# PSUM tiles of one bank, values loaded first, and stores issued from ScalarE, in a pooled-attention and mixture-of-depths kernel

## The chip, the cores and the metric

The kernel runs on one core of one Trainium2 chip. The metric is the device time of one execution in microseconds. The core has a matrix engine (TensorE, "PE" in the profile, with "PEld" for its weight loads), VectorE (DVE), ScalarE (ACT), GpSimd (POOL) and SyncE (SP), each with its own in-order queue. Matmuls write to PSUM, a memory of eight banks of 512 float32 values in each of 128 partitions; everything else is in SBUF. SP, ACT and POOL can issue transfers (DMAs).

## What is computed

Eight batches of an attention with pooled keys and values, followed by a feed-forward block that only the best 128 of 576 rows pass through. In short:

```python
# q, k, v: (8, 8, 576, 64)
k_p = k.reshape(B, H, 72, 8, D).mean(axis=3); v_p = v.reshape(B, H, 72, 8, D).mean(axis=3)
scores = scale * q @ k_p^T                       # per head (576, 72)
attn = softmax(scores);  x = attn @ v_p          # bridged to x: (8, 576, 512)
# mixture of depths, per batch
s = x @ w_gate                                   # (576,)
top = the 128 rows of largest s
h = relu(x[top] @ w1);  y = h @ w2               # 512 -> 1024 -> 512
out = x;  out[top] = x[top] + sigmoid(s[top]) * y
```

## The kernel before

`direct_path` is what runs (`general_path` is code for inputs out of range and is skipped). Per batch there are these stages, each with its name in the code and the engine it is on:

- Loads of k, q and v from SP (`load`, line 285 for all DMAs of SP). The values are folded in halves: of the 128 partitions of the tile `vr`, 112 are plain and 16 get a second key's rows added by an accumulating DMA that POOL issues (line 367).
- Pooling of k (L380, L381) and its transposition and that of q on DVE (L386 to L401); pooling of v, with the gate's product and sum (L443 to L455).
- `scores` (L419): four groups t of matmuls into the PSUM tile `pS`; `ex` (L429) takes the exponential into `et`.
- `attend` (L470): five groups c of matmuls into two banks of the PSUM tile `pB` (one bank for c = 4). `zs` (L485, L486, ACT) copies the row sums out, `norm` (L492, L493, DVE) divides and writes `xs`; then `xs` is stored to the output (32 stores of 256 KB, 16 of 64 KB).
- `rank`: the row scores are transposed on PE (`spread`, L542), copied by ACT (L547), compared on DVE (five times L554), turned into one-hot rows (L559); a matmul (`pick`, L568) gives the row numbers, DVE reads them (L573, L574), POOL makes indices (L578) and gathers the chosen rows from the stored output (L579).
- `dense`: `turn` (L596) transposes them, ACT copies (L598), `up` (L605) is 64 pieces of the first product in two halves g, `relu` (L610, ACT) follows each half, `down` (L614) the second product, `end` (L619, DVE) the sum, `put` (L623, POOL) scatters the rows.

The order of all work on each engine is written out before the program is built. Every stage calls `add` with a cost, what it reads and writes, a priority and, for PSUM, the banks it may take; `Plan.place` runs a small model of the five engines, picks at each step the ready stage of the best priority, and sorts all by the modelled start. Waits between engines are then put in by the framework, which follows each tile. A DMA of SP or ACT also uses one of eight semaphores (DMAHW0 to DMAHW7) in turn, and is issued only after the DMA that used the same semaphore before it has landed.

`pB` is one tile of four banks: 0 and 1 for the attends, 2 and 3 for the jobs (spread, pick, turn, up, down). `pS` is one tile of four banks, in which the plan sees two slots of 128 columns, both in each of the banks.

Of the kernel before, what the change touches and what calls it, by code (L numbers as in the profile page):

```python
# [165 lines left out]
def direct_path(ctx, tc, q, k, v, moe_w_gate, moe_w1, moe_w2, moe_capacity, out, flag):  # L166
# [11 lines left out]
    NC = 5  # L178
# [84 lines left out]
    pB = psum.tile([128, 4, 512], FT, name="pB")  # L263
# [28 lines left out]
    def opening():  # L292
# [51 lines left out]
    def load_kq(b):  # L344
        p = 100 * b
        src = k[b].rearrange("h (g t) d -> (h g) t d", g=G)
        cuts = ((0, 20), (20, 36)) if b == 0 else ((0, 36),)
        for n, (a, z) in enumerate(cuts):
            load(KR[:, a:z], src[:, a:z], 128 * 256 * (z - a), p + n,
                (), [("KR", n)] if b == 0 else [("KR", 0), ("KR", 1)])  # L350
        src = q[b].rearrange("h (g t) d -> (h g) t d", g=G)
        for h, (a, z) in enumerate(HALF):
            load(QR[b % 2][h], src[:, a:z], 128 * 256 * (z - a), p + 2, (), [("QR", b % 2, h)])

    def load_v(b):
        p = 100 * b + 3
        i = b % 2
        x = VR[i]

        def rows(key, n, step):  # L360
            return bass.AP(tensor=v.tensor, offset=v.offset + b * H * S * D + key * W * D,
                           ap=[[step * W * D, n], [S * D, H], [1, W * D]])
        load(x[TWO:128], rows(TWO, 128 - TWO, 2), (128 - TWO) * 8192, p, (), [("VRb", i)])
        load(x[0:TWO], rows(0, TWO, 1), TWO * 8192, p, (), [("VRa", i)])

        def more():
            nc.gpsimd.dma_start(out=x[TWO:128], in_=rows(TWO + 1, 128 - TWO, 2), accum_op=OP.add)  # L367
        add("POOL", 1.0, more, (), [("VRb", i)], p - 100, nbytes=(128 - TWO) * 8192)
# [89 lines left out]
    def attend(b, c):  # L458
        i = b % 2
        et = ET[c][b % NB[c]]  # L460
        slot = ("acc", b, c)
        vkeys = [(x, i, n) for x in ("VPd", "VPg") for n in range(2)]

        def go():
            bank = plan.bank[slot][0]
            for s in range(2):
                for m in range(NP):
                    for u in range(ROWS[c] // 64):
                        w, d, y = (u, s, m) if c < 4 else (m // 2, 0, 2 * s + m % 2)
                        nc.tensor.matmul(pB[64 * w : 64 * w + 64, bank + d, E * y : E * y + E],  # L470
                                         et[:, 2 * m + s, 64 * u : 64 * u + 64], VP[i][:, 2 * m + s, :], start=True, stop=True)
        add("PE", 1.05 if c < 4 else 0.6, go, [("ET", c, b % NB[c])] + vkeys, [slot], 100 * b + 5 + c,
            takes=(slot, ((ACC2 if b < 2 else ACC) if c < 4 else (ONE2 if b < 2 else ONE))))
# [3 lines left out]
        def acc():  # L477
            bank = plan.bank[slot][0]
            if c < 4:
                return pB[:, bank : bank + 2, 0 : NP * E].rearrange("p s (m d) -> p s m d", d=E)  # L480
            return pB[:, bank, 0 : NP * E].rearrange("p (s m d) -> p s m d", s=2, d=E)

        def zs():
            o = acc()
            nc.scalar.activation(ZA[:, b, z0 : z0 + nz].rearrange("p (s m) -> p s m", s=2), o[:, :, :, D], AF.Identity, bias=eps)  # L485
            nc.scalar.copy(out=SS[i][:, c, 0:nz].rearrange("p (s m) -> p s m", s=2), in_=o[:, :, :, D + 1])  # L486
        add("ACT", 0.45, zs, [slot], [("Z", b, c), ("SS", i, c)], 100 * b - 35)

# [13 lines left out]
        if c < 4:  # L502
            dma(rows[:, TC * c : TC * c + TC], XS[i][c], 128 * 2048, 100 * b + 4,
                [("XS", i, c)], [("ROWS", b, c, 0)], then=kept)
        else:
            for w in range(2):
                dma(rows[:, TC * c : TG, 256 * w : 256 * w + 256], XS[i][c][64 * w : 64 * w + 64],
                    64 * 1024, 100 * b + 4, [("XS", i, c)], [("ROWS", b, c, w)], then=kept)

    def rank(b):  # L510
# [23 lines left out]
        for half, (a, z) in enumerate(((0, 3), (3, NC))):  # L534
# [11 lines left out]
            def keep(a=a, w=w, slot=slot):  # L546
                nc.scalar.copy(out=SR[:, OFF[a] : OFF[a] + w], in_=pB[:, plan.bank[slot][0], 0:w])  # L547
# [16 lines left out]
        def pick():  # L564
            bank = plan.bank[slot][0]
            for c in range(NC):
                n = ROWS[c]
                nc.tensor.matmul(pB[0:cap, bank, 0:5], OH[0:n, c, :], AUX[i][0:n, c, :], start=(c == 0), stop=(c == NC - 1))  # L568
        add("PE", 0.4, pick, ["OH", ("AUX", i)], [slot], p - 70, takes=(slot, JOB))

        def token():
            got = pB[0:cap, plan.bank[slot][0]]
# [4 lines left out]
        def index():  # L577
# [6 lines left out]
            [("IX", x), ("XR", x)], p - 90, nbytes=262144, mark=b)  # L584
# [4 lines left out]
    def dense(b):  # L589
# [4 lines left out]
        def turn():  # L594
            for d in range(DB):
                nc.tensor.transpose(pB[:, plan.bank[ts][0], cap * d : cap * d + cap], XR[x][:, 128 * d : 128 * d + 128], ident[:cap, :cap])  # L596
        add("PE", 0.55, turn, [("XR", x), "ident"], [ts], p - 15, takes=(ts, JOB))
        add("ACT", 0.6, lambda: nc.scalar.copy(out=XG[i].rearrange("p d n -> p (d n)"), in_=pB[:, plan.bank[ts][0], 0 : DB * cap]),  # L598
            [ts], [("XG", i)], p - 5000, gives=(ts,))
        for g in range(2):  # L600
            for f in range(FB // 2):
                def up(f=f, g=g):
                    bank = plan.bank[us[g]][0]
                    for d in range(DB):
                        nc.tensor.matmul(pB[:, bank, cap * f : cap * f + cap], w1[g][:, d, 128 * f : 128 * f + 128],  # L605
# [3 lines left out]
            def relu(g=g):  # L609
                nc.scalar.activation(HT[i][g].rearrange("p f n -> p (f n)"), pB[:, plan.bank[us[g]][0], 0 : FB // 2 * cap], AF.Relu)  # L610
            add("ACT", 0.65, relu, [us[g]], [("HT", i, g)], p - 5000, gives=(us[g],))
        for f in range(FB):
            def down(f=f):
                nc.tensor.matmul(pB[0:cap, plan.bank[ds][0], :], HT[i][f // 4][:, f % 4, :], w2[f // 4][:, f % 4, :],  # L614
# [3 lines left out]
        def end():  # L618
            nc.vector.scalar_tensor_tensor(Y[i], pB[0:cap, plan.bank[ds][0], :], GV[x], XR[x], op0=OP.mult, op1=OP.add)  # L619
# [7 lines left out]
        add("POOL", 1.1, put, [("Y", i), ("IX", x)], [("OUT", b)], p - 5000, nbytes=262144, mark=b)  # L627
# [9 lines left out]
    def range_test():  # L637
# [11 lines left out]
        add("PE", 0.2, lambda: nc.tensor.matmul(pB[0:1, plan.bank[slot][0], 0:2], ones, seen, start=True, stop=True),  # L649
            ["seen0", "seen1", "ones"], [slot], 2050, takes=(slot, JOB))  # L650

        def verdict():
            nc.vector.scalar_tensor_tensor(match, pB[0:1, plan.bank[slot][0], 0:2], 1.0, want, op0=OP.mult, op1=OP.is_equal, accum_out=good)
# [16 lines left out]
    for b in range(2):  # L670
        load_kq(b)
        load_v(b)
        if b == 0:
            load_gate()
        else:
            weights()
        front(b)
    for b in range(B):
        dense(b)
        if b + 2 < B:  # L680
            load_kq(b + 2)
            load_v(b + 2)
# [359 lines left out]
```

## Time and profile before

| | us |
|---|---|
| three runs | 357.27, 348.56, 357.25; median 357.25 |
| profiled execution | 351.87 |
| its span, first to last instruction | 350.1 |

The profile gives for each engine when an instruction ran and what ended the idle time before it. A name such as `xs L493` is the instruction of that line that writes `xs`. A wait for several semaphores is put down to the one that came last. The granted clock of TensorE is given as a share of full speed: 1.00 is 2.4 GHz, 0.50 is 1.2 GHz.

### The profile page before, as it was taken

The numbers are of one execution on the slowest core, as the hardware profiler recorded it, in microseconds if no ns is written. First come the engines' busy times: TensorE is split into PE (matmuls) and PEld (weight loads), VectorE is DVE, ScalarE is ACT, GpSimd is POOL, SyncE is SP. The second block draws the span as 40 slices with busy tenths as digits, with TensorE's granted clock in tenths as the row PEclk, the third lists the DMA queues.
The fourth block names the chain that finished last, engine by engine and source line by source line (L and its number), as shares of the span: only waits on it lengthen the run. The fifth ranks groups of instructions, "written<-read, shape, count | busy, mean of one in ns | idle before, by whom it ended". The sixth has DMA issues, their size and how long they took to land. (4 is left out here: it accounts for less than half of the span.)

```text
span 350.1 us, 6979 instructions
## 1 busy us (share of the span) xinstructions
PE 246.8 (70%) x2942; PEld 180.4 (52%) x2942; DVE 147.2 (42%) x323; ACT 72.1 (21%) x178; POOL 111.2 (32%) x166
## 2 busy tenths in 40 slices
PE   8546620969677886767686886766857887979890
PEld 3435610858543765633575653653446637464740
DVE  7473269576444885374564136124322151000000
ACT  1313030344112533120244311022010101010000
POOL 2104068857490856553541211110020002010101
PEclk9965875899899999999999999898965999999996
DMA  8999997979825938815421210311121001000000
GB/s 287 291 261 309 404 288 281 222 254 278 301 59 133 323 94 224 301 33 128 139 51 40 84 47 31 91 47 31 30 91 38 9 0 61 2 30 0 32 6 33
DMA packets 22663, 46.93 MB, mean 134 GB/s; under 512 B 1888, under 2 KB 12128, under 8 KB 21728
## 3 DMA queue, kind: packets, MB, share of 16 engines
q1 hardware_dynamic: 20192, 41.16, 38.7%
q0 software_dynamic: 2432, 5.24, 5.9%
q8 instruction: 25, 0.41, 0.5%
q14 instruction: 14, 0.11, 0.1%
HBM read 34.87 MB, written 11.53 MB: 133 GB/s over the span
## 5 line engine op out<-in xcount | busy, mean ns | idle before, releaser
L605 PE MATMUL pB<-xg,w 128*128 128x128 f32 x512 | 74.1, 299 | 21.9 <-DVE xs L493 13.1
L605 PEld LDWEIGHTS pB<-xg,w 128*128 128x128 f32 x512 | 65.8, 206 | 29.8 <-DVE xs L493 16.2
L614 PE MATMUL pB<-w,ht 128*128 128x512 f32 x128 | 63.8, 624 | 12.8 <-ACT ht L610 4.3
L470 PE MATMUL pB<-vp,et 128*64 128x66 f32 x1152 | 46.1, 237 | 15.8 <-DVE xs L493 8.0
L419 PE MATMUL pS<-qt,kt 32*128 32x128 f32 (+1 forms) x1024 | 43.7, 319 | 17.6 <-ACT et L429 11.4
L470 PEld LDWEIGHTS pB<-vp,et 128*64 128x64 f32 x1152 | 40.9, 149 | 23.9 <-DVE xs L493 9.0
L554 DVE SCALAR_TENSOR_TENSOR cmp<-sr,sc,lat 128x576 bf16<-128x576 f32 (+1 forms) x40 | 41.8, 1044 | 21.2 <-ACT sr L547 20.0
L419 PEld LDWEIGHTS pS<-qt,kt 32*128 32x128 f32 x1024 | 37.9, 208 | 22.5 <-ACT et L429 14.3
L429 ACT ACTIVATE et<-pS 128x1024 f32<-128x1024 f32 (+1 forms) x40 | 36.6, 942 | 40.5 <-PE pS L419 40.5
L614 PEld LDWEIGHTS pB<-w,ht 128*128 128x128 f32 x128 | 22.2, 193 | 43.0 <-issue 16.5
L493 DVE TENSOR_TENSOR xs<-pB,rz 128x512 f32<-128x512 f32 (+1 forms) x40 | 25.5, 638 | 24.7 <-PE pB L614 9.3
L492 DVE RECIPROCAL rz<-za 128x8 f32<-128x8 f32 (+1 forms) x40 | 7.8, 196 | 66.5 <-ACT za L485 66.4
L623 POOL DMA_INDIRECT out_dram<-y,ix x8 | 8.7, 1091 | 71.4 <-DVE y L619 51.1
L619 DVE SCALAR_TENSOR_TENSOR y<-pB,gv,xr 128x512 f32<-128x512 f32 x8 | 6.0, 749 | 51.1 <-PE pB L605 19.2
L485 ACT ACTIVATE za<-pB,eps 128x8 f32<-128x8 f32 (+1 forms) x40 | 10.7, 268 | 79.4 <-PE pB L605 35.9
L380 POOL TENSOR_TENSOR kr<-kr 128x640 f32<-128x640 f32 (+1 forms) x12 | 18.4, 1534 | 13.5 <-DMA kr<-in_k_dram 13.5
L443 POOL TENSOR_TENSOR vr<-vr 128x512 f32<-128x512 f32 x15 | 21.3, 1420 | 2.6 <-DMA vr<-in_v_dram 2.6
L401 DVE STREAM_TRANSPOSE qt<-qr 128x1024 f32<-128x1024 f32 (+1 forms) x16 | 21.7, 1366 | 0.4 <-DMA qr<-in_q_dram 0.4
L610 ACT ACTIVATE ht<-pB 128x512 f32<-128x512 f32 x16 | 9.6, 597 | 57.7 <-PE pB L605 32.0
L578 POOL TENSOR_SCALAR ix<-tk 128x1 int32<-128x1 f32 x8 | 2.3, 289 | 58.2 <-DVE gv L574 50.5
L527 POOL CAST aux<-sc 128x5 bf16<-128x5 f32 x8 | 1.6, 198 | 44.8 <-DVE sc L522 44.8
L367 POOL DMA_DIRECT2D vr<-in_v_dram x8 | 7.8, 979 | 21.5 <-DMA vr<-in_v_dram 21.4
(74 smaller groups left out, 172.2 us busy)
## 6 DMA issues: line engine op xcount, KB each, us to landing
out_dram<-xs SPq DMA_DIRECT2D x32, 256.0 KB, 3.4
kr<-in_k_dram SPq DMA_DIRECT2D x7, 1152.0 KB, 11.3
vr<-in_v_dram SPq DMA_DIRECT2D x8, 896.0 KB, 7.7
qr<-in_q_dram SPq DMA_DIRECT2D x8, 640.0 KB, 8.8
qr<-in_q_dram SPq DMA_DIRECT2D x8, 512.0 KB, 10.8
w<-in_moe_w_dram SPq DMA_DIRECT2D x4, 1024.0 KB, 17.8
vr<-in_v_dram SPq DMA_DIRECT2D x8, 128.0 KB, 3.6
vr<-in_v_dram POOLq DMA_DIRECT2D x8, 128.0 KB, 8.3
```

The costliest lines, as they stand in the source:

```text
L380: e.tensor_tensor(out=x[:, a:z, 0:2], in0=x[:, a:z, 0:2], in1=x[:, a:z, 2:4], op=OP.add)
L401: nc.vector.transpose(out=QT[b % 2][h].rearrange("p j s (t g) -> p t (j s) g", g=G), in_=QR[b % 2][h].rearrange("p t (j s g) -> p t (j s) ...
L419: nc.tensor.matmul(pS[:, i, 256 * s + y : 256 * s + y + n], KT[b % 2][p, j, s, :], QT[b % 2][h][p, j, s, x : x + n], start=(j == 0), stop= ...
L429: nc.scalar.activation(ET[c][b % NB[c]].rearrange("p n (g t) -> p n g t", g=G), pS.rearrange("p i (s x) -> p (i s) x", s=2)[:, :, y : y + ...
L443: e.tensor_tensor(out=x[:, a:z, 0:2], in0=x[:, a:z, 0:2], in1=x[:, a:z, 2:4], op=OP.add)
L470: nc.tensor.matmul(pB[64 * w : 64 * w + 64, bank + d, E * y : E * y + E], et[:, 2 * m + s, 64 * u : 64 * u + 64], VP[i][:, 2 * m + s, :], ...
L485: nc.scalar.activation(ZA[:, b, z0 : z0 + nz].rearrange("p (s m) -> p s m", s=2), o[:, :, :, D], AF.Identity, bias=eps)
L493: nc.vector.tensor_tensor(out=XS[i][c].rearrange("p (m s d) -> p s m d", s=2, d=D), in0=o[:, :, :, 0:D], in1=rz.rearrange("p (s m one) -> ...
L554: nc.vector.scalar_tensor_tensor(cmp[0:n], SR[0:n], SC[i][0:n, c : c + 1], LAT[0:n, LAST - OFF[c] : LAST - OFF[c] + S], op0=OP.subtract, o ...
L605: nc.tensor.matmul(pB[:, bank, cap * f : cap * f + cap], w1[g][:, d, 128 * f : 128 * f + 128], XG[i][:, d, :], start=(d == 0), stop=(d == ...
L610: nc.scalar.activation(HT[i][g].rearrange("p f n -> p (f n)"), pB[:, plan.bank[us[g]][0], 0 : FB // 2 * cap], AF.Relu)
L614: nc.tensor.matmul(pB[0:cap, plan.bank[ds][0], :], HT[i][f // 4][:, f % 4, :], w2[f // 4][:, f % 4, :], start=(f == 0), stop=(f == FB - 1))
```

## The change

Three things are changed, and the plan's description of them with them.

PSUM: `pB` is split into `pA` (two banks, one tile, for the attends) and `pJ0`, `pJ1` (one bank each, for the jobs). The plan sees four slots: 0 is `pA`, 1 and 2 are the jobs, 3 is the whole of `pS`, so one group of scores at a time. In batches 0 and 1 an attend may also take both job banks; c = 4 may take `pA` or a job bank. Where an attend lies in two tiles, `zs` and `norm` are issued once for each.

Loads: the values' small piece comes first in each batch, then k, then q and the rest of v (for batch 0 v before q). The plan sees the accumulating DMA with another cost.

Stores: the stores of `xs` are issued by ACT, with a priority ahead of the loads' old place; the plan gives them a cost of 0.3 on ACT and no bytes.

```diff
-    plan.free = {x: 0.0 for x in range(6)}
-    SIDE, BOTH = [(4,), (5,)], [(4, 5)]
-    ACC, ACC2 = [(0, 1)], [(0, 1), (2, 3)]
-    ONE, ONE2 = [(0,), (1,)], [(0,), (1,), (2,), (3,)]
-    JOB = [(2,), (3,)]
+    plan.free = {x: 0.0 for x in range(4)}
+    ACC, ACC2 = [(0,)], [(0,), (1, 2)]
+    ONE = [(0,), (1,), (2,)]
+    JOB = [(1,), (2,)]
+    SIDE = [(3,)]
...
-    pB = psum.tile([128, 4, 512], FT, name="pB")
+    pA = psum.tile([128, 2, 512], FT, name="pA")
+    pJ = [psum.tile([128, 512], FT, name=f"pJ{i}") for i in range(2)]
...
-        return add(eng, 0.06 if eng == "SP" else 1.0, go, reads, writes, prio, nbytes=nbytes, after=after)
+        if eng == "SP":
+            return add(eng, 0.06, go, reads, writes, prio, nbytes=nbytes, after=after)
+        return add(eng, 0.3, go, reads, writes, prio, late=2.5, after=after)
...
-        add("POOL", 1.0, more, (), [("VRb", i)], p - 100, nbytes=(128 - TWO) * 8192)
+        add("POOL", 1.0, more, (), [("VRb", i)], 100 * b - 97, late=4.0)
...
-            y = off()
-                        nc.tensor.matmul(pS[:, i, 256 * s + y : 256 * s + y + n], KT[b % 2][p, j, s, :],
+                        nc.tensor.matmul(pS[:, i, 256 * s : 256 * s + n], KT[b % 2][p, j, s, :],
-            takes=(slot, SIDE if t < 3 else BOTH))
+            takes=(slot, SIDE))
...
-            takes=(slot, ((ACC2 if b < 2 else ACC) if c < 4 else (ONE2 if b < 2 else ONE))))
+            takes=(slot, ((ACC2 if b < 2 else ACC) if c < 4 else ONE)))
...
-            dma(rows[:, TC * c : TC * c + TC], XS[i][c], 128 * 2048, 100 * b + 4,
-                [("XS", i, c)], [("ROWS", b, c, 0)], then=kept)
+            dma(rows[:, TC * c : TC * c + TC], XS[i][c], 128 * 2048, 100 * b - 30,
+                [("XS", i, c)], [("ROWS", b, c, 0)], then=kept, eng="ACT")
...
-            [("IX", x), ("XR", x)], p - 90, nbytes=262144, mark=b)
+            [("IX", x), ("XR", x)], p - 90, late=3.5, mark=b)
...
-    for b in range(2):
-        load_kq(b)
-        load_v(b)
-        if b == 0:
-            load_gate()
-        else:
-            weights()
-        front(b)
+    load_v1(0)
+    load_k(0)
+    load_v2(0)
+    load_q(0)
+    load_gate()
+    front(0)
+    load_v1(1)
+    load_k(1)
+    load_q(1)
+    load_v2(1)
+    weights()
+    front(1)
```

The change moves work on every engine. Three places follow; line numbers of the changed kernel are some lines higher (L470 becomes L478, L605 becomes L615, L614 becomes L624, L419 becomes L424, L485 becomes L495, L429 becomes L434).

On PE, the attends of batch 2 and the down pieces of batch 0 among them, before (`vp0` and `et` belong to batch 2, `ht00` and `ht01` are the two halves of batch 0's hidden rows; in brackets the engines or DMA semaphores that the row waits for):

```order
L470 MATMUL pB_160<-vp0_90,et20_86 64x66 x16
L614 MATMUL pB_160<-w20_143,ht00_135 128x512 [waits DMAHW6_49,Activation_49]
L614 MATMUL pB_160<-w20_143,ht00_135 128x512 [waits Activation_49]
L614 MATMUL pB_160<-w20_143,ht00_135 128x512 [waits DVE_49]
L470 MATMUL pB_160<-vp0_90,et30_88 64x66 x16
L614 MATMUL pB_160<-w20_143,ht00_135 128x512
L614 MATMUL pB_160<-w21_144,ht01_136 128x512 [waits DMAHW7_49,DVE_49]
L470 MATMUL pB_160<-vp0_90,et40_89 64x66 x8
```

And in the changed kernel:

```order
L624 MATMUL pJ1_162<-w20_143,ht00_135 128x512
L478 MATMUL pA_160<-vp0_90,et10_84 64x66 [waits DVE_49]
L478 MATMUL pA_160<-vp0_90,et10_84 64x66 x15
L424 MATMUL pS_159<-qt01_79,kt0_76 128x192 [waits Activation_49]
L424 MATMUL pS_159<-qt01_79,kt0_76 128x192 x15
L624 MATMUL pJ1_162<-w21_144,ht01_136 128x512 [waits DMAHW1_49]
L478 MATMUL pA_160<-vp0_90,et20_86 64x66 [waits DVE_49]
L478 MATMUL pA_160<-vp0_90,et20_86 64x66 x15
L624 MATMUL pJ1_162<-w21_144,ht01_136 128x512
L478 MATMUL pJ0_161<-vp0_90,et40_89 64x66 [waits Activation_49]
```

The waits for DVE and ACT stood at the down pieces, and now stand at the attends and the scores.

On POOL, the first batches' values, before (`vr0`, `vp0` are batch 0's, `vr1` batch 1's; the two DMAs are the accumulating ones):

```order
L367 DMA vr0_72<-in_v_dram 16x8x256 [waits DMAHW4_49]
L367 DMA vr1_73<-in_v_dram 16x8x256 [waits DMAHW2_49]
L443 TENSOR_TENSOR vr0_72<-vr0_72 128x4x128 [waits DMAHW5_49,DMASW0_49]
L451 TENSOR_TENSOR vr0_72<-vp0_90,wg_92 128x4x64 [waits DMAHW6_49,DVE_49]
L447 TENSOR_TENSOR vp0_90<-vr0_72 128x4x64 [waits Pool_49]
```

And in the changed kernel:

```order
L372 DMA vr0_72<-in_v_dram 16x8x256 [waits DMAHW0_49]
L448 TENSOR_TENSOR vr0_72<-vr0_72 128x4x128 [waits DMAHW3_49,DMASW0_49]
L452 TENSOR_TENSOR vp0_90<-vr0_72 128x4x64 [waits Pool_49]
L456 TENSOR_TENSOR vr0_72<-vp0_90,wg_92 128x4x64 [waits DMAHW6_49,DVE_49]
L456 TENSOR_TENSOR vr0_72<-vp0_90,wg_92 128x4x64 [waits Pool_49]
L372 DMA vr1_73<-in_v_dram 16x8x256 [waits DMAHW7_49]
```

Batch 1's accumulating DMA has moved from ahead of batch 0's pooling to behind it.

On ACT, the end of batch 0's attention, before (`et01` is batch 1's first exponential, `sr` the copy for batch 0's rank):

```order
L485 ACTIVATE za_145<-pB_160,eps_146 128x4 [waits DVE_49,PE_49]
L486 COPY ss0_103<-pB_160 128x4
L429 ACTIVATE et40_89<-pS_159 128x512 [waits Activation_49]
L518 COPY ss0_103<-ss0_103 64x4 [waits DVE_49,Activation_49]
L547 COPY sr_112<-pB_160 128x384 [waits PE_49]
```

And in the changed kernel:

```order
L289 DMA out_0_dram<-xs03_96 16x8x512 [waits DMAHW4_49,DVE_49]
L434 ACTIVATE et01_83<-pS_159 128x1024 [waits PE_49]
L528 COPY ss0_103<-ss0_103 64x4 [waits DVE_49,Activation_49]
L289 DMA out_0_dram<-xs04_97 16x4x256 [waits DMAHW6_49]
L289 DMA out_0_dram<-xs04_97 16x4x256 [waits DMAHW0_49]
L434 ACTIVATE et11_85<-pS_159 128x1024 [waits PE_49]
L557 COPY sr_112<-pJ0_161 128x384 [waits PE_49]
```

Stores now stand between the exponentials, each behind a DMA semaphore: DMAHW4, DMAHW6 and DMAHW0 were last used by the first three of the four weight loads.

## Rows read from the trace of the kernel before

**Rows 1.** Windows, PE alone: stretch, length, PE busy (instructions), granted clock, DMA.
```profile
0.00:81.87 81.87, 46.66 (x832) 0.79 0.96 290
81.87:342.05 260.18, 200.12 (x2115) 0.95 0.30 88
255.00:275.00 20.00, 14.68 (x101) 0.57 0.20 60
```

**Rows 2.** Waits of PE: line, waited for: us in total, times, longest.
```profile
PE pB L605 <- DVE xs L493: 13.1, 11, 1.5
...
PE pB L614 <- ACT ht L610: 4.3, 6, 0.7
PE pB L605 <- ACT ht L610: 3.5, 5, 0.7
...
PE pB L614 <- DVE xs L493: 3.1, 3, 1.5
PE pB L568 <- DVE xs L493: 3.0, 3, 1.4
PE pB L614 <- ACT ss L486: 2.9, 7, 0.4
PE pB L542 <- DVE xs L493: 2.8, 3, 1.3
PE pB L470 <- ACT ht L610: 2.7, 4, 0.7
PE pB L596 <- DVE xs L493: 2.6, 2, 1.5
...
PE pB L470 <- DVE y L619: 2.3, 2, 1.5
...
PE pB L596 <- DVE gv L574: 0.4, 1, 0.4
```

**Rows 3.** Waits of PE again: scores on the exponential.
```profile
PE pS L419 <- ACT et L429: 11.4, 10, 2.1
```

**Rows 4.** Timeline of PE, 222 to 230: start, us, instruction, [idle before, releaser].
```profile
224.97 1.15 PE L470 MATMUL pB<-vp,et 128*64 128x66 f32 x32
226.05 1.16 PE L605 MATMUL pB<-xg,w 128*128 128x128 f32 x8
228.70 1.16 PE L605 MATMUL pB<-xg,w 128*128 128x128 f32 x8 [1.49 <-DVE xs L493]
```

**Rows 5.** Timeline of ACT, the same stretch.
```profile
227.25 0.27 ACT L485 ACTIVATE za<-pB,eps 128x8 f32<-128x8 f32 x1 [4.50 <-PE pB L605]
```

**Rows 6.** Timeline of DVE, the same stretch.
```profile
227.95 0.69 DVE L493 TENSOR_TENSOR xs<-pB,rz 128x512 f32<-128x512 f32 x1 [0.20 <-DVE rz L492]
```

**Rows 7.** Timeline of the opening, all engines, 0 to 60.
```profile
10.70 17.21 SPq L285 DMA_DIRECT2D w<-in_moe_w_dram  x4
11.00 1.45 POOL L367 DMA_DIRECT2D vr<-in_v_dram  x1 [8.25 <-DMA vr<-in_v_dram]
...
25.64 0.88 POOL L367 DMA_DIRECT2D vr<-in_v_dram  x1 [13.18 <-DMA vr<-in_v_dram]
26.24 1.57 POOL L443 TENSOR_TENSOR vr<-vr 128x512 f32<-128x512 f32 x1
...
36.83 2.26 PE L470 MATMUL pB<-vp,et 128*64 128x66 f32 x64
```

**Rows 8.** Timeline of PE from 59: first pick, first up pieces.
```profile
60.34 0.38 PE L568 MATMUL pB<-aux,oh 128*128 128x5 bf16 x5 [8.26 <-DVE oh L559]
...
81.87 2.05 PE L605 MATMUL pB<-xg,w 128*128 128x128 f32 x16
```

**Rows 9.** The page's groups: a comparison of the rank.
```profile
L554 DVE SCALAR_TENSOR_TENSOR cmp<-sr,sc,lat 128x576 bf16<-128x576 f32 (+1 forms) x40 | 41.8, 1044 | 21.2 <-ACT sr L547 20.0
```

**Rows 10.** Timeline of SP: one load's issue.
```profile
50.37 0.53 SPq L285 DMA_DIRECT2D kr<-in_k_dram  x1
```

**Rows 11.** DMA issues: KB each, us to landing.
```profile
qr<-in_q_dram SPq DMA_DIRECT2D x8, 512.0 KB, 10.8
```

More of the change, by code (lines that the diff above doesn't have):

```diff
@@ L262, in direct_path, with job @@
     pS = psum.tile([128, NP, 512], FT, name="pS")
-    pB = psum.tile([128, 4, 512], FT, name="pB")
+    pA = psum.tile([128, 2, 512], FT, name="pA")
+    pJ = [psum.tile([128, 512], FT, name=f"pJ{i}") for i in range(2)]
+    def job(slot):
+        return pJ[plan.bank[slot][0] - 1]
     out_rows = out.rearrange("b s d -> (b s) d")
@@ L461, in attend, with banks @@
         slot = ("acc", b, c)
+        def banks():
+            x = plan.bank[slot]
+            return [pJ[y - 1] for y in x] if x[0] else [pA[:, 0], pA[:, 1]]
         vkeys = [(x, i, n) for x in ("VPd", "VPg") for n in range(2)]
         def go():
-            bank = plan.bank[slot][0]
+            o = banks()
             for s in range(2):
@@ L538, in spread @@
             def spread(a=a, z=z, slot=slot):
-                bank = plan.bank[slot][0]
+                row = job(slot)
                 for c in range(a, z):
                     n = ROWS[c]
-                    nc.tensor.transpose(pB[:, bank, OFF[c] - OFF[a] : OFF[c] - OFF[a] + n],
+                    nc.tensor.transpose(row[:, OFF[c] - OFF[a] : OFF[c] - OFF[a] + n],
                                         SC[i][0:n, c : c + 1].to_broadcast([n, 128]), ident[0:n, 0:n])
@@ L546, in keep @@
             def keep(a=a, w=w, slot=slot):
-                nc.scalar.copy(out=SR[:, OFF[a] : OFF[a] + w], in_=pB[:, plan.bank[slot][0], 0:w])
+                nc.scalar.copy(out=SR[:, OFF[a] : OFF[a] + w], in_=job(slot)[:, 0:w])
             add("ACT", 0.2 + 0.8e-3 * w, keep, [slot], [("SR", half)], p - 70, gives=(slot,))
@@ L595, in turn @@
             for d in range(DB):
-                nc.tensor.transpose(pB[:, plan.bank[ts][0], cap * d : cap * d + cap], XR[x][:, 128 * d : 128 * d + 128], ident[:cap, :cap])
+                nc.tensor.transpose(job(ts)[:, cap * d : cap * d + cap], XR[x][:, 128 * d : 128 * d + 128], ident[:cap, :cap])
         add("PE", 0.55, turn, [("XR", x), "ident"], [ts], p - 15, takes=(ts, JOB))
-        add("ACT", 0.6, lambda: nc.scalar.copy(out=XG[i].rearrange("p d n -> p (d n)"), in_=pB[:, plan.bank[ts][0], 0 : DB * cap]),
+        add("ACT", 0.6, lambda: nc.scalar.copy(out=XG[i].rearrange("p d n -> p (d n)"), in_=job(ts)[:, 0 : DB * cap]),
             [ts], [("XG", i)], p - 5000, gives=(ts,))
@@ L609, in relu @@
             def relu(g=g):
-                nc.scalar.activation(HT[i][g].rearrange("p f n -> p (f n)"), pB[:, plan.bank[us[g]][0], 0 : FB // 2 * cap], AF.Relu)
+                nc.scalar.activation(HT[i][g].rearrange("p f n -> p (f n)"), job(us[g])[:, 0 : FB // 2 * cap], AF.Relu)
             add("ACT", 0.65, relu, [us[g]], [("HT", i, g)], p - 5000, gives=(us[g],))
@@ L613, in down @@
             def down(f=f):
-                nc.tensor.matmul(pB[0:cap, plan.bank[ds][0], :], HT[i][f // 4][:, f % 4, :], w2[f // 4][:, f % 4, :],
+                nc.tensor.matmul(job(ds)[0:cap, :], HT[i][f // 4][:, f % 4, :], w2[f // 4][:, f % 4, :],
                                  start=(f == 0), stop=(f == FB - 1))
@@ L618, in end @@
         def end():
-            nc.vector.scalar_tensor_tensor(Y[i], pB[0:cap, plan.bank[ds][0], :], GV[x], XR[x], op0=OP.mult, op1=OP.add)
+            nc.vector.scalar_tensor_tensor(Y[i], job(ds)[0:cap, :], GV[x], XR[x], op0=OP.mult, op1=OP.add)
         add("DVE", 0.75, end, [ds, ("GV", x), ("XR", x)], [("Y", i)], p - 5000, gives=(ds,))
@@ L626, in put @@
             scat[b] = [j]
-        add("POOL", 1.1, put, [("Y", i), ("IX", x)], [("OUT", b)], p - 5000, nbytes=262144, mark=b)
+        add("POOL", 1.1, put, [("Y", i), ("IX", x)], [("OUT", b)], p - 5000, late=3.0, mark=b)
     def weights():
@@ L648, in range_test @@
         slot = ("seen",)
-        add("PE", 0.2, lambda: nc.tensor.matmul(pB[0:1, plan.bank[slot][0], 0:2], ones, seen, start=True, stop=True),
+        add("PE", 0.2, lambda: nc.tensor.matmul(job(slot)[0:1, 0:2], ones, seen, start=True, stop=True),
             ["seen0", "seen1", "ones"], [slot], 2050, takes=(slot, JOB))
         def verdict():
-            nc.vector.scalar_tensor_tensor(match, pB[0:1, plan.bank[slot][0], 0:2], 1.0, want, op0=OP.mult, op1=OP.is_equal, accum_out=good)
+            nc.vector.scalar_tensor_tensor(match, job(slot)[0:1, 0:2], 1.0, want, op0=OP.mult, op1=OP.is_equal, accum_out=good)
             nc.vector.tensor_scalar(flag, good, 1.5, None, op0=OP.is_lt)
```

75 lines of the change are left out of this document (39 added, 36 removed).

## The prediction

> **What bounds the kernel now.** I read the windows of PE first, then its waits, then single places of the timeline. The windows cut the profiled execution where the first up piece of a dense stage runs, at 81.87. Before it the transfers are busy almost all the time (0.96 of the DMA engines, 290 GB/s) and PE works 46.7 of 81.9 us; behind it transfers fall to 0.30, PE is busy 200.1 of 260.2 us, and it is PE's order that sets the end: 60.1 us of that stretch is PE standing still [rows 1]. So two questions decide: how early the first dense stage can start, and what PE waits for in those 60 us.
>
> PE's waits answer the second. An up piece (L605) writes to bank 2 or 3 and reads weights and gathered rows; it has no business with `xs`, which DVE makes from banks 0 and 1. Yet it waits for it eleven times, 13.1 us. The same holds for eight more rows: down pieces that wait for a hidden half they don't read, jobs that wait for the sums' copy, attends that wait for the relu. The nine largest come to 38.0 us, and there are twelve smaller ones from 2.3 down to 0.4, 14.4 us together [rows 2]. The timeline shows how such a wait comes about. An attend runs at 224.97 and an up piece behind it until 227.21 [rows 4]. ScalarE's reading of the attend's sums starts at 227.25, when the up piece is over, though the attend ended a piece earlier [rows 5]; DVE's division ends at 228.64 [rows 6]; then the next up piece starts, after 1.49 us of idling [rows 4]. Readers wait for a writer of another bank, and writers for a reader of another bank, in turn. With the four banks in three tiles none of these waits has a cause, and the order of PE in the changed kernel has none of them: its waits stand at the attends and scores.
>
> Of PSUM the trace shows only the waits, not a need for them. The Trainium skill, PSUM — Partial Sum Buffer, section "PSUM bank collisions raise a hardware error", asks for semaphores by bank and quadrant; by that rule the 52.4 us are the program's own and the chip needs none of them, and the sum below would stay as it is. No run here shows more than that the waits are there.
>
> **The opening.** In the profile POOL issues batch 0's accumulating DMA at 11.00, then stands 13.18 us for batch 1's small piece of values, and pools batch 0 only at 26.24; the first attend runs at 36.83 [rows 7]. The changed order takes that second DMA out of the way and loads the values first. 2.2 MB then stand ahead of the pooling, 7.7 us at 290 GB/s [rows 1], and the accumulating DMA is issued at some 4 instead of 11.00; had it as long to go as from 11.00 to 26.24 (15.2 us), it is there at 19, without the queue in front of it at 10. I take 15, and the first attend at 18 to 19: 18 us sooner.
>
> Not all of that arrives. The stores are now in ScalarE's queue. Those of batch 0's last group wait for the semaphores of the second and third weight load, and behind them stand batch 1's second exponential and the copy of the row scores for batch 0's rank. That SP is held in this way now is seen where four issues of weights take 17.21 us [rows 7]; one issue alone is 0.53 [rows 10]. Up to the third weight load 10.8 MB have to land: 37 us at 290 GB/s. So the copies are done at about 39 to 40; five comparisons at 1.04 us [rows 9] and the one-hot, costed as one more, bring the pick to 46, against 60.34 [rows 8]. From the pick to the first up piece it is 21.5 us now [rows 8], because PE's order has other work there; in the changed order there stand two attends of batch 1, its spread (which waits for the last division) and the turn; I cost that at 10: two attends of 1.15 [rows 4] with their chains of reading and dividing (1.4 each, from the start in rows 5 to the end in rows 6), and spread, its copy, turn and its copy as four pieces of 1.16 [rows 4]. First up piece at 56, 26 us sooner. From this goes work that PE has now done by 81.87 and then hasn't: three groups of scores and an attend of batch 2, each of 32 matmuls and costed at 1.15 us as the attend of rows 4, 5 us in all. **Term one: −21**, with bounds −10 (values late) and −26.
>
> **The waits: −52.4.** All of rows 2 go. What is late next is the true order: an attend into `pA` still waits for the division of the one before, since there is one such slot. The chain of reading and dividing is 1.4 us [rows 5, 6] and at least one piece of 1.16 [rows 4] usually stands between, so 0.3 us stay, four times in each of six batches: **+7**, with bounds 0 and 24 × 1.4 = 34. Scores now get one slot in place of two. I cost that at nothing: they wait for the exponential already, 11.4 us [rows 3], so two slots in the same banks gave no overlap; the plan now knows it and puts other pieces there. If it does not, the 11.4 stay.
>
> **The stores: +8.** 48 stores leave SP, where nothing waited for their issue, and go to ScalarE. No row shows ScalarE issuing a DMA. SP's 0.53 [rows 10] is the nearest row; 36 stores lie behind the opening, 19 us of ScalarE. Below, an idle ScalarE makes it 0; above, all 19 reach PE. I charge a quarter, 5. Then the landing: of the 48 stores, 24 wait in the changed order for a semaphore last used by a load. The plan gives ScalarE's stores no transfer, so it doesn't see that. Loads run ahead of PE by two batches, so I charge one place, the end of batch 2, where the store waits for batch 4's values: 3.
>
> A rule that speaks against this part: the Trainium skill, DMA: Bandwidth & Descriptors, section "Issuing engines are not separate DMA queues", says that transfers from different engines end up on the same 16 DMA engines, and issuing from another one only saves sequencer time. By it the stores gain nothing and the two charges stand alone; the sum has it so. No row here shows a ScalarE transfer to compare.
>
> **The clock: −4.** Between 255 and 275 the granted clock is 0.57, PE being partly idle before; 14.7 us of work there would be 8.4 at full speed [rows 1]. With fewer gaps I take most of it back; bounds 0 and −6.3. Split `zs` and `norm` in batches 0 and 1 add a few instructions on engines that are waiting then: nothing; were they on the path, less than 1 us a piece, inside the bounds.
>
> **Sum.** 351.9 (the profiled execution's own time) − 21 − 52.4 + 7 + 8 − 4 = **289.5**. That execution is 1.5% under the median of the runs shown, 357.25; I do not scale the forecast, but lean up within its range. 289.5 it is, and 272 to 308 for this case alone: the bounds of the opening and half of those of the attends and stores.
>
> **Rivals.**
> - *The wait changes its owner.* One attend slot, one scores slot: if no piece stands between, each attend pays the full 1.4 (+34 instead of +7) and the 11.4 of scores stay. For it: rows 3. Against it: the changed order has a job piece between most attends. 289.5 + 27 + about 5 of the 11.4 not yet in it = 321. Chance 0.13.
> - *The opening stays bound by transfers.* Values come at 19 and the rank waits for the weights' landing later than 37; then term one is −5 and the time 305. For it: 0.96 of the DMA engines busy [rows 1]. Chance 0.08.
> - *ScalarE's queue becomes the bound: slower.* Place: the 24 stores that wait for a load, with exponentials, sums and relus queued behind them. A load takes 10.8 us to land [rows 11]; if each store meets half of one, 5.4, and all of it reaches PE, it is 130 us, less the 8 charged: 411. It is slower than before from (351.9 − 289.5 + 8) / 24 = 2.9 us a store. For it: nothing in the plan models it. Against it: loads run two batches ahead, DMA is 0.30 busy behind 81.87 [rows 1]. Chance 0.05.
> - *The framework still joins the tiles*, and the change only moves the opening: 331. Against it speaks PE's order. Chance 0.02.
>
> My forecast has the rest, 0.72. The range of eight in ten: from 270 to 322, which takes in the first two rivals. A difference of about 2% (7 us) is what a measurement of this kernel can tell. Faster by over 2%: 0.92; within 2%: 0.03; slower: 0.05, the third rival.
>
> **What the changed profile would show.** Opening: POOL pools batch 0's values before 19, first pick near 46, first up piece near 56. Waits: no row of L615 or L624 on `xs` or the sums; attends (L478) on `xs` at 0.3 each; PE's idle time behind the first up piece near 25 instead of 60. Stores: ScalarE held once near 37, by a load of weights, and hardly later. I am wrong if ScalarE stands behind transfers in the middle of the kernel, if attends wait over 1 us each, or if the first up piece comes after 70.

## The result, and the profile after

The changed kernel takes 275.52 us (median of four runs, 273.09 to 279.09), against 352.9 for the kernel before on the same chip (344.74 to 357.27): ratio 0.7925, 95% interval 0.778 to 0.807. Forecast were 289.5, with 270 to 322. All ratios here leave out disturbed runs of either kernel, so they differ a little from the quotient of the medians. The profiled execution of after has 275.98, 75.9 less than the one of before with 351.87.

The windows of PE, cut at the first up piece as in [rows 1] and at PE's last work (columns: length, busy time and instructions by engine, granted clock, DMA share, GB/s):

```profile
0.00:59.01 59.01, 36.08 (x576) 27.21 (x576) 41.85 (x98) 17.27 (x46) 22.98 (x47) 0.85 0.99 304
59.01:266.10 207.09, 195.90 (x2367) 149.23 (x2367) 112.81 (x228) 57.18 (x138) 90.92 (x119) 0.96 0.45 139
```

PE stands still for 22.9 us before the first up piece, 35.2 in [rows 1]; and for 11.2 us behind it, 60.1 in [rows 1]. Its busy time is 232.0, against 246.8. The differences, 12.3 + 48.9 + 14.8 = 76.0, are the whole 75.9 but for rounding.

All that PE waits for (total, times, longest), cut behind the tenth of 14 rows:

```profile
PE pS L424 <- DVE qt L410: 8.9, 2, 7.5
PE pA L478 <- DVE xs L503: 4.6, 3, 2.4
PE pJ L552 <- DVE sc L532: 3.8, 1, 3.8
PE pS L424 <- ACT et L434: 3.5, 3, 1.8
PE pJ L606 <- DMA xr<-out_dram,ix: 3.2, 2, 2.6
PE pJ L552 <- ACT sr L557: 2.8, 1, 2.8
PE pS L307 <- DVE fours L314: 1.5, 1, 1.5
PE pJ L615 <- ACT xg L608: 1.3, 2, 0.7
PE pA L478 <- ACT et L434: 1.1, 1, 1.1
PE pJ L478 <- ACT et L434: 1.1, 1, 1.1
```

L615 and L624 are up and down now. No row has one of them waiting for `xs`, the sums or a hidden half: [rows 2] are gone. What an attend and the work around it look like, in PE's, ScalarE's and DVE's timeline:

```profile
138.47 1.15 PE L478 MATMUL pA<-vp,et 128*64 128x66 f32 x32
139.55 1.58 PE L424 MATMUL pS<-qt,kt 32*128 32x192 f32 x32
141.06 1.16 PE L615 MATMUL pJ<-xg,w 128*128 128x128 f32 x8
142.15 1.15 PE L478 MATMUL pA<-vp,et 128*64 128x66 f32 x32
```
```profile
139.91 0.27 ACT L495 ACTIVATE za<-pA,eps 128x8 f32<-128x8 f32 x1 [2.22 <-PE pA L478]
141.20 1.02 ACT L434 ACTIVATE et<-pS 128x1024 f32<-128x1024 f32 x1 [0.97 <-PE pS L424]
141.34 0.55 ACTq L289 DMA_DIRECT2D out_dram<-xs  x1
```
```profile
140.61 0.69 DVE L503 TENSOR_TENSOR xs<-pA,rz 128x512 f32<-128x512 f32 x1 [0.20 <-DVE rz L501]
```

The sums are read at 139.91, 0.3 us after the attend's end at 139.62, where [rows 4, 5] had the reader wait for the next piece as well. DVE divides until 141.30 while PE goes on; the next attend starts at 142.15 without a wait.

The opening, in POOL's and PE's timeline:

```profile
3.86 1.15 POOL L372 DMA_DIRECT2D vr<-in_v_dram  x1 [1.10 <-DMA vr<-in_v_dram]
13.81 1.75 POOL L448 TENSOR_TENSOR vr<-vr 128x512 f32<-128x512 f32 x1 [8.81 <-DMA vr<-in_v_dram]
```
```profile
17.06 2.09 PE L424 MATMUL pS<-qt,kt 32*128 32x128 f32 x32 [7.49 <-DVE qt L410]
22.31 1.91 PE L478 MATMUL pA<-vp,et 128*64 128x66 f32 x32
48.45 0.36 PE L578 MATMUL pJ<-aux,oh 128*128 128x5 bf16 x5
57.24 1.09 PE L606 MATMUL pJ<-ident,xr 128*128 128x128 f32 x4 [0.63 <-DMA xr<-out_dram,ix]
59.01 1.22 PE L615 MATMUL pJ<-xg,w 128*128 128x128 f32 x4 [0.68 <-ACT xg L608]
```

Against [rows 7, 8]: the accumulating DMA at 3.86 (11.00), the pooling at 13.81 (26.24), the first attend at 22.31 (36.83), the pick at 48.45 (60.34), the first up piece at 59.01 (81.87). Forecast were 4, 15, 18 to 19, 46 and 56.

One place in the middle, the end of batch 2, in ScalarE's, POOL's and PE's timeline:

```profile
87.85 5.15 ACTq L289 DMA_DIRECT2D out_dram<-xs  x2
93.04 1.02 ACT L434 ACTIVATE et<-pS 128x1024 f32<-128x1024 f32 x1 [5.32 <-DVE kh L395]
93.96 0.47 ACT L557 COPY sr<-pJ 128x384 f32<-128x384 f32 x1
```
```profile
92.51 1.26 POOL L448 TENSOR_TENSOR vr<-vr 128x512 f32<-128x512 f32 x1 [1.68 <-DMA vr<-in_v_dram]
94.49 0.52 PE L552 MATMUL pJ<-ident,sc 128*128 128x128 f32 x2 [2.80 <-ACT sr L557]
```

Two stores of batch 2 take 5.15 us to issue, where two issues take 1.1 (ACTq is ScalarE's queue of DMA issues). The second needs DMAHW2, which batch 4's large piece of values used last; POOL waits for the same landing and goes on at 92.51. Behind the store stand an exponential (its wait is put down to DVE, but the issue ends last, at 93.00) and the copy of batch 2's row scores, and PE waits 2.80 us for that copy.

### The profile page after: what moved, and what is told of

It reads as the page before. It is cut to its first block, busy times and chain, and to the rows that moved or that the text cites. A ratio compares the mean times of both kernels' runs of the same rounds, so it can differ in the third digit from the quotient of the medians.

```text
span 274.2 us, 6966 instructions
## 1 busy us (share of the span) xinstructions
PE 232.2 (85%) x2942; PEld 176.4 (64%) x2942; DVE 155.4 (57%) x326; ACT 74.5 (27%) x184; POOL 114.9 (42%) x166
## 3 DMA queue, kind: packets, MB, share of 16 engines
q1 hardware_dynamic: 14304, 31.72, 36.1%
## 5 line engine op out<-in xcount | busy, mean ns | idle before, releaser
L615 PE MATMUL pJ<-xg,w 128*128 128x128 f32 x512 | 66.8, 290 | 1.8 <-ACT xg L608 1.3
L615 PEld LDWEIGHTS pJ<-xg,w 128*128 128x128 f32 x512 | 63.0, 203 | 5.5 <-ACT xg L608 2.2
L624 PE MATMUL pJ<-w,ht 128*128 128x512 f32 x128 | 61.0, 606 | 0.0
L424 PE MATMUL pS<-qt,kt 32*128 32x128 f32 (+1 forms) x1024 | 46.6, 322 | 12.9 <-DVE qt L410 8.9
L434 ACT ACTIVATE et<-pS 128x1024 f32<-128x1024 f32 (+1 forms) x40 | 36.9, 939 | 61.0 <-PE pS L424 51.3
L424 PEld LDWEIGHTS pS<-qt,kt 32*128 32x128 f32 x1024 | 39.0, 207 | 21.8 <-DVE qt L410 9.9
L478 PEld LDWEIGHTS pA<-vp,et 128*64 128x64 f32 x944 | 31.7, 143 | 14.4 <-DVE xs L503 6.0
L478 PE MATMUL pA<-vp,et 128*64 128x66 f32 x944 | 35.8, 231 | 5.8 <-DVE xs L503 4.6
L624 PEld LDWEIGHTS pJ<-w,ht 128*128 128x128 f32 x128 | 22.2, 190 | 19.9 <-issue 18.4
L503 DVE TENSOR_TENSOR xs<-pA,rz 128x512 f32<-128x512 f32 (+1 forms) x30 | 20.5, 683 | 4.8 <-DVE rz L501 2.2
L620 ACT ACTIVATE ht<-pJ 128x512 f32<-128x512 f32 x16 | 9.6, 598 | 44.9 <-PE pJ L615 44.9
L495 ACT ACTIVATE za<-pA,eps 128x8 f32<-128x8 f32 (+1 forms) x30 | 8.0, 268 | 26.8 <-PE pA L478 23.8
L552 PE MATMUL pJ<-ident,sc 128*128 128x128 f32 (+1 forms) x40 | 8.9, 317 | 6.6 <-DVE sc L532 3.8
L452 POOL TENSOR_TENSOR vp<-vr 128x256 f32<-128x256 f32 x15 | 12.3, 818 | 3.3 <-PE pA L478 2.7
## 6 DMA issues: line engine op xcount, KB each, us to landing
qr<-in_q_dram SPq DMA_DIRECT2D x8, 640.0 KB, 11.2
vr<-in_v_dram SPq DMA_DIRECT2D x8, 128.0 KB, 10.9
```

Source lines behind the costliest of these rows:

```text
L424: nc.tensor.matmul(pS[:, i, 256 * s : 256 * s + n], KT[b % 2][p, j, s, :], QT[b % 2][h][p, j, s, x : x + n], start=(j == 0), stop=(j == 1))
L452: e.tensor_tensor(out=VP[i][:, a:z, 0:D], in0=x[:, a:z, 0], in1=x[:, a:z, 1], op=OP.add)
L478: nc.tensor.matmul(o[d][64 * w : 64 * w + 64, E * y : E * y + E], et[:, 2 * m + s, 64 * u : 64 * u + 64], VP[i][:, 2 * m + s, :], start=Tr ...
L615: nc.tensor.matmul(acc[:, cap * f : cap * f + cap], w1[g][:, d, 128 * f : 128 * f + 128], XG[i][:, d, :], start=(d == 0), stop=(d == DB - 1))
L624: nc.tensor.matmul(job(ds)[0:cap, :], HT[i][f // 4][:, f % 4, :], w2[f // 4][:, f % 4, :], start=(f == 0), stop=(f == FB - 1))
```

## The experiments

My theory: the joined tile made the waits and its border is most of the gain; the loads' order is a gain of its own; the stores are worth nothing. The rivals: the order that follows from the plan's new slots brings the gain; the stores' move brings part of it, by freeing SP, or costs what I had charged. Experiments 1 and 9, and the two runs of the PSUM part with tiles apart and joined, keep the order of every engine. In the others the plan writes another order along with the edit, and the run measures both.

**1. The tiles joined again.** The order of all engines stays as in the changed kernel.

```diff
-    pA = psum.tile([128, 2, 512], FT, name="pA")
-    pJ = [psum.tile([128, 512], FT, name=f"pJ{i}") for i in range(2)]
+    pB = psum.tile([128, 4, 512], FT, name="pB")
+    pA, pJ = pB[:, 0:2], [pB[:, 2], pB[:, 3]]
```

> The changed kernel with its four banks for accumulator and jobs declared as one tile again, and pA, pJ0 and pJ1 as parts of it; slots, plan, order of all engines, loads and stores as in the changed kernel. Theory (the joined tile made the waits): the waits between banks come back. PE stood still 60.1 us behind the first up piece before and 11.2 us in the changed kernel; with the same order I expect some 45 of these 49 us back, so 276 + 45 = 321 us, between 305 and 335, with up pieces waiting for xs and down pieces for hidden halves they do not read. Rival (the order that comes from the plan's truer list of banks brings the gain, and the tiles' names nothing): under 283 us.

Measured: 338.68 us, ratio 0.9643 (0.950 to 0.979). That is 63 us back, more than the 45 of the idle time, and above the range that I gave. Its windows, and some of PE's waits:

```profile
0.00:65.31 65.31, 39.29 (x575) 30.11 (x576) 43.10 (x98) 17.01 (x46) 23.42 (x47) 0.76 0.92 274
65.31:328.93 263.62, 213.03 (x2367) 153.68 (x2367) 107.02 (x228) 57.12 (x138) 90.44 (x119) 0.94 0.36 109
```
```profile
PE pB L624 <- DVE xs L503: 9.3, 9, 1.5
PE pB L615 <- DVE xs L503: 4.4, 5, 1.5
PE pB L615 <- ACT ht L620: 3.5, 5, 0.7
PE pB L624 <- ACT ht L620: 2.9, 4, 0.7
```

Behind the first up piece the same 2367 matmuls have 50.6 us of idle time (11.2 in the changed kernel) and 213.0 us of busy time (195.9). So a wait costs more than the time it stands for. The last down stage, here and then in the changed kernel, both at a granted clock of 1.00, shows a part of it (the three down stages before it show the same):

```profile
320.88 1.02 PE L624 MATMUL pB<-w,ht 128*128 128x512 f32 x2
322.65 6.28 PE L624 MATMUL pB<-w,ht 128*128 128x512 f32 x14 [0.75 <-ACT ht L620]
```
```profile
259.27 7.03 PE L624 MATMUL pJ<-w,ht 128*128 128x512 f32 x16
```

Sixteen matmuls take 7.03 in one run and 1.02 + 6.28 = 7.30 in two, beside 0.75 of waiting: 0.27 for one interruption. Another part is the clock. Summing busy time times (1 − granted clock) over slices of 5 us, PE lost 23.8 us to a lower clock here, 12.9 in the changed kernel and 18.5 before.

**2. The stores back on SP.**

```diff
-            dma(rows[...], XS[i][c], 128 * 2048, 100 * b - 30, ..., then=kept, eng="ACT")
+            dma(rows[...], XS[i][c], 128 * 2048, 100 * b + 4, ..., then=kept)
```

> The changed kernel with the 48 stores of attention rows issued by SP again, with the priority they had before. Theory (the stores' move is worth nothing either way; I had charged it 8 us and the changed trace shows ScalarE held for 2 to 3 us in the opening only): 270 to 279 us. Rival A (the move brought part of the gain, as a store that waits for its rows no longer holds the loads behind it on SP): 285 us or more, with the loads of later batches issued later. Rival B (the charge of 8 was right): 268 us or less.

Measured: 276.21 us, ratio 0.7892 (0.783 to 0.796): no difference from the changed kernel, so in the total the charge of 8 us had nothing to it here. ScalarE is not held in the opening only: the two stores from 87.85 on held it for some 4 us. With the stores on SP, PE's wait of 2.80 us for the copy is gone, but in the new order other waits stand in its place: PE is idle for 36.6 us before its last work, 34.1 in the changed kernel.

**3. The loads in the old order**, stores on ScalarE.

```diff
-    load_v1(0); load_k(0); load_v2(0); load_q(0)
+    load_kq(0); load_v(0)          # and so for each batch
-        add("POOL", 1.0, more, (), [("VRb", i)], 100 * b - 97, late=4.0)
+        add("POOL", 1.0, more, (), [("VRb", i)], p - 100, nbytes=(128 - TWO) * 8192)
```

> The changed kernel with the loads in the order of before (keys, queries, values of a batch, the small piece of values ahead of the large one) and the accumulating DMA planned as a transfer again. Theory (the opening is a gain of its own, 21 us in my sum): first attend after 33 us instead of 22.3, first up piece at 75 to 82 instead of 59.0, and 276 + 18 = 294 us, between 288 and 300. Rival (the opening gets better by itself once PSUM's tiles are apart): first up piece before 67, under 283 us.

Measured: 287.36 us, ratio 0.8232 (0.817 to 0.829), 12 us more, with the first attend at 35.37 and the first up piece at 72.37, between theory and rival. But the rows are about ScalarE:

```profile
38.88 5.18 ACTq L289 DMA_DIRECT2D out_dram<-xs  x2
44.10 0.27 ACT L492 ACTIVATE za<-pA,eps 128x8 f32<-128x8 f32 x1 [5.88 <-DMA qr<-in_q_dram]
50.45 3.62 ACTq L289 DMA_DIRECT2D out_dram<-xs  x2
54.12 0.70 ACT L554 COPY sr<-pJ 128x384 f32<-128x384 f32 x2 [5.33 <-DMA kr<-in_k_dram]
```

Two pairs of stores, 5.18 and 3.62 us where two issues take 1.1, wait for loads that have to land; the reading of sums and the copy of the row scores stand behind them. This is the mechanism of my third rival, in the opening, where I had looked for it behind the weights' loads. So I could not tell yet what the loads' order is worth by itself.

**4. Batch 0's queries first.**

```diff
-    load_v2(0)
     load_q(0)
+    load_v2(0)
```

> The changed kernel with batch 0's queries loaded ahead of the large piece of its values. In the changed trace the first scores wait 7.49 us for DVE's transposition of the queries, which stands behind the pooling of values, and run at 17.06; before they ran at 10.41. Theory (they are on the path of the opening): first scores near 11, first attend at 19 to 21, first up piece near 56, 273 us. Rival (DVE's work for batch 1 sets the opening's end, between 26.5 and 36): first scores near 11 but first up piece at 58 to 60, 275 to 277 us.

Measured: 273.06 us, ratio 0.7816 (0.776 to 0.787). The first scores run at 11.34, the first attend at 18.91, the first up piece at 57.53. It is the lowest of all versions, but its interval overlaps with that of the changed kernel, so I do not call it faster.

**5 to 8. Each part alone.** The PSUM part alone is the changed kernel with the edits of experiments 2 and 3 together; the plan alone has that of experiment 1 as well. The loads' part and the stores' part are each put into the kernel before:

```diff
 (loads)  -    for b in range(2): load_kq(b); load_v(b); ...
          +    load_v1(0); load_k(0); load_v2(0); load_q(0); ...
 (stores) -            dma(rows[...], XS[i][c], 128 * 2048, 100 * b + 4, ..., then=kept)
          +            dma(rows[...], XS[i][c], 128 * 2048, 100 * b - 30, ..., then=kept, eng="ACT")
```

> Of the three parts the PSUM one alone: four tiles and the slots that go with them (and the plan's costs of the accumulating DMA aside, all of its numbers), loads in the order of before, stores on SP. Theory (joined tiles made the waits; their worth is by far the largest part; stores are worth nothing): as the changed kernel with the old loads, 284 to 292 us, which is 60 to 66 under the kernel before. Rival (the parts only pay together): over 300 us.

> The run of the PSUM part alone, with the four banks joined in one tile again: only the plan's new list of slots, and so the order, is left. Theory (the order does not help while readers and writers of different banks wait for each other): 344 to 354 us, no different from before. Rival (the order is a good part of the gain: one slot for scores, one pair for attends): under 335 us.

> The kernel before with the new order of loads and the accumulating DMA's new cost alone. Theory (the loads' order is worth some 12 us, as the run of the changed kernel with the old loads says, and this does not hang on the tiles): 337 to 344 us. Rival (my term of 21 us for the opening holds in the kernel before): 326 to 333 us.

> The kernel before with the 48 stores issued by ScalarE alone. Theory (worth nothing, with ScalarE 27% busy in the changed kernel): 347 to 356 us. Rival (it costs what I had charged, and more while PE waits for ScalarE's reading of the sums): 358 us or more.

| kernel | median us | ratio to before (95%) |
|---|---|---|
| PSUM part alone | 278.06 | 0.8043 (0.798 to 0.811) |
| its plan and order, tiles joined | 343.96 | 0.9842 (0.975 to 0.994) |
| loads alone | 359.80 | 1.0320 (1.016 to 1.048) |
| stores alone | 355.75 | 1.0316 (1.025 to 1.039) |

The PSUM part alone is nearly the whole result, more than I had expected of it. The other two parts, each alone, bring no gain: loads alone is outside both of my ranges, and stores alone inside the theory's. By the ratios each is 3% slower, but the runs behind these two ratios had granted clocks of 0.90 to 0.91, those of the kernel before 0.92 to 0.93; at 0.88 to 0.89 the kernel before took 354 to 359 us on the same chip. So it is not shown that the parts themselves cost the 3%. The windows of the PSUM part alone:

```profile
0.00:73.48 73.48, 46.63 (x699) 36.95 (x699) 46.69 (x105) 19.82 (x49) 31.27 (x52) 0.70 1.01 314
73.48:267.53 194.05, 184.43 (x2248) 139.32 (x2244) 102.47 (x222) 54.05 (x137) 81.52 (x114) 1.00 0.41 121
```

Its first up piece comes 14.5 us later than in the changed kernel, and its end only 1.4 us later (267.53 against 266.10), since PE has done 10.6 us more work by then. Idle time is 26.9 and 9.6 us: 36.5 in all, 34.1 in the changed kernel.

In the loads alone the earliness is lost on the way. PE's timeline:

```profile
50.87 0.37 PE L571 MATMUL pB<-aux,oh 128*128 128x5 bf16 x5
72.26 0.38 PE L571 MATMUL pB<-aux,oh 128*128 128x5 bf16 x5 [6.40 <-DVE oh L562]
78.76 0.66 PE L599 MATMUL pB<-ident,xr 128*128 128x128 f32 x4
82.00 2.05 PE L608 MATMUL pB<-xg,w 128*128 128x128 f32 x16
```

Batch 0's pick runs 9.5 us earlier than in [rows 8], but the order puts its turn behind batch 1's pick, and the first up piece stands at 82.00, where it stood at 81.87. That explains why nothing is gained.

With the tiles apart the two parts act together:

| tiles apart | stores on SP | stores on ScalarE |
|---|---|---|
| old loads | 0.8043 (0.798 to 0.811) | 0.8232 (0.817 to 0.829) |
| new loads | 0.7892 (0.783 to 0.796) | 0.7925 (0.778 to 0.807) |

The stores cost 2.3% with the old loads and nothing measurable with the new; the new loads are worth 1.9% with stores on SP by these ratios, but 0.7% by the medians (278.06 and 276.21, on two chips), and PE's idle time is the same, 36.5 and 36.6 us. So their gain with stores on SP is not shown. Both together, against the PSUM part alone, can't be told from nothing.

**9. The accumulator apart, the two job banks joined.**

```diff
-    pJ = [psum.tile([128, 512], FT, name=f"pJ{i}") for i in range(2)]
+    pJ2 = psum.tile([128, 2, 512], FT, name="pJ")
+    pJ = [pJ2[:, 0], pJ2[:, 1]]
```

> The changed kernel with pA a tile of its own, and the two banks of the jobs joined in one tile; all else as in the changed kernel. It tells which of the three borders carries the gain. In the trace of the run with all four banks joined, PE's waits that go across the two job banks alone (up and down pieces for hidden halves, gathered rows, the output rows, the row of scores) come to some 17 us of its 39 us of added idle time. Theory (each false wait costs its idle time and some 0.3 us more of PE's records, and the two borders share the gain about by half): 290 to 302 us. Rival A (the accumulator's border is all that matters): 274 to 281 us. Rival B (waits taken from one border go over to the other): 315 us or more.

Measured: 302.92 us, ratio 0.8767 (0.861 to 0.893), just above what the theory gave. Its waits have the hidden halves again, and not `xs`:

```profile
PE pJ L616 <- ACT ht L621: 3.5, 5, 0.7
PE pJ L625 <- ACT ht L621: 2.9, 4, 0.7
PE pJ L616 <- DVE y L630: 2.4, 2, 1.5
```

From 338.68 the accumulator's border is worth 36 us, and from 302.92 the border between the jobs 27. By the ratios, which allow for the different chips, it is 0.088 and 0.084 of the time before, about half each. Neither alone is the cause.

**10 and 11. Towards a shorter opening.** With the queries first, ScalarE's queue stands for 4.00 us before batch 0's last stores. All stores, or batch 0's six, go to SP in turn, by the edit of experiment 2 and by `eng="ACT" if b else "SP"`.

> Batch 0's queries loaded ahead of its large piece of values, and all 48 stores on SP. With the queries first, ScalarE's queue stands at 32.07 for 4.00 us before two stores that wait for the weights' semaphores, and the copy behind them waits 7.07 us. Theory (this is on the path of the opening): ScalarE not held, first pick some 3 us earlier than 47.3, 268 to 272 us. Rival (SP's stores hold later loads as much as they held ScalarE): 272 to 276 us.

> Batch 0's queries loaded ahead of its large piece of values, and batch 0's six stores on SP, the other 42 on ScalarE. Theory (the hold of ScalarE at 32.07, 4.00 us, is on the path, and later stores cost nothing on ScalarE): 268 to 271 us, the best of all versions. Rival (nothing waits for it in the end, PE having other work): 272 to 275 us, as with the queries first alone.

Measured: 275.83 (0.7959, 0.776 to 0.816) and 276.18 us (0.7956, 0.783 to 0.809). The first is in its rival's range, the second 1 us above its rival's: neither shortens the kernel. With all stores on SP the pick did come earlier, 6.4 us before that of the changed kernel, and the first up piece 1.8:

```profile
42.07 0.36 PE L578 MATMUL pJ<-aux,oh 128*128 128x5 bf16 x5
57.25 5.49 PE L615 MATMUL pJ<-xg,w 128*128 128x128 f32 x24 [0.68 <-ACT xg L608]
```

It had 22.1 us of idle time before that piece and 14.0 behind it, 36.1 together, so nothing was won.

## Why the prediction came out right, and which of its terms did not

Forecast and measured, term by term; measured are differences of PE's windows between the two profiled executions:

| term | forecast | measured |
|---|---|---|
| opening | −21 | −12.3 of idle time |
| false waits gone, new waits, stores | −52.4 + 7 + 8 = −37.4 | −48.9 of idle time |
| PE's busy time (clock) | −4 | −14.8 |
| sum | −62.4 | −76.0 |

- **The bound was right.** PE's order sets the end, and its waits across banks were the cause. Joining the tiles alone, in the same order, brings 63 us back; the plan's order with joined tiles gains 1.6%. My rival that the tiles stay joined for the framework falls with the waits.
- **The false waits, −52.4: right in idle time.** The PSUM part alone takes 50.5 us of idle time out behind the first up piece (60.1 to 9.6). In the kernel before, 51.9 of the 52.4 us stand there, and 8.2 of other waits; in the changed kernel 11.2 are left in all. So some 3 us were new, where 7 + 8 had been charged. Not every one of the smaller rows was false: an up piece reads the copy of the gathered rows, and L615 still waits for it, 1.3 us.
- **The new waits, +7, were charged too high.** Attends wait for a division three times, 4.6 us, two of them in the opening, against my 24 times 0.3. That is over 1 us each, which I had called a sign of being wrong; but other work nearly always stands between two attends, so there are only three. The single slot for scores, charged at nothing, cost nothing: their wait for the exponential fell from 11.4 to 3.5. The first rival, each attend paying 1.4 us, did not happen.
- **The stores, +8: the landing right, the issues charged for nothing.** Of the 5 for issues no row shows anything; the row at 141.34 above shows one issue inside ScalarE's activation of 141.20 to 142.22, which takes 1.02 us as the one at 93.04 does without. The 3 for a landing were charged to the end of batch 2, where a store waits for batch 4's values, and there it is: 2.80 us of PE's waiting, with ScalarE standing behind a transfer in the middle of the kernel, which I had called a sign of being wrong. It is one place. In the total the move is worth 0 with the new loads; with the old loads, where two more such holds stand in the opening, it costs 9 us. The third rival's mechanism exists; its price of 5.4 us for each of 24 stores does not. The Trainium skill, DMA: Bandwidth & Descriptors, section "Issuing engines are not separate DMA queues", would have had the move gain nothing but the issuer's time; the two runs with new loads agree (0.7892 and 0.7925).
- **The opening, −21: the term that was wrong.** The first up piece did come 22.9 us earlier. The step that failed is what was set against it, "5 us in all" of work that PE had done by 81.87. It was 46.7 − 36.1 = 10.6 us: I had counted three groups of scores and an attend, and it was seven groups of scores and an attend. The scores before the cut, before and then in the changed kernel (the windows' second number is PE's busy time):

```profile
0.00:81.87 81.87, 23.01 (x480) 20.07 (x480) 0.79 0.96 290
0.00:59.01 59.01, 13.53 (x256) 11.43 (x256) 0.85 0.99 304
```

  And of the 12.3 us that are left, the PSUM part alone gives 8.3 (26.9 idle instead of 35.2). Part of that is the tiles: joining them again brings 3.1 us of idle time back before the first up piece in the changed kernel's order (26.0 in experiment 1, against 22.9) and 5.9 in the order of the PSUM part (32.8 against 26.9), where attends then wait 8.7 us for `xs`. The rest is the plan's order. The new loads and stores together give the other 4.0, of which 1.6 come back behind the first up piece (11.2 against 9.6). I had also counted the shorter way from pick to up piece, 21.5 to 10.6, in this term. With the old loads and the stores on ScalarE it is 72.37 − 60.78 = 11.6: it belongs to the plan's order and not to the loads.
- **The clock, −4: too small.** PE's busy time fell by 14.8. Some 5.6 of it (18.5 − 12.9) is the clock, within my bounds; the other 9 I had no term for. Interruptions are the candidate: PE waits 95 times before and 21 times in the changed kernel. At 0.27 each the 74 that went would be 20 us, so 0.27 is not the price of every one, and the cause of this share stays open.

So the total came within 14 us in part by luck: one gain was put too high by 8.7, and two costs and the gain of the clock were sized wrong the other way.

## What to carry to other kernels

Look for waits between instructions that share a tile and no data, above all where PE's rows name a reader of another bank: each costs its idle time, an interruption, and perhaps the clock. Measure an earlier opening by PE's idle time before a cut, not by when a late piece first runs; if PE fills the time with other work, the earlier piece is worth little. Before a DMA is moved to a compute engine, ask which earlier transfer its semaphore waits for and what stands behind it in that queue.

## What the runs showed of the hardware that was not expected

ScalarE's issue of a DMA is recorded at 0.55 us, SP's at 0.53 [rows 10], and it runs beside ScalarE's own activation. In the last four down stages of experiment 1 an interruption of a run of matmuls costs 0.27 us beside its wait, at a granted clock of 1.00. All that a wait costs beside itself came to 20 us of busy time in experiment 1: 252.3 against 232.2 over the whole execution, of it 10.9 the clock (23.8 − 12.9).
